# A fused attention and FFN kernel: batch 0 worked in token halves with gated loads, the first FFN block in halves, and the last output tile in two column pieces

## Chip, core and metric

The kernel runs on one core of one Trainium2 chip. The metric is the device time of one execution in microseconds (us); the median of several runs is compared. Profiles are of one execution each. Engines are named as in the profile: PE (matmul; PEld its weight loads), DVE (vector), ACT (scalar), POOL (GpSimd), SP (which issues most DMAs).

## What is computed

```python
# q, k, v: (8, 8, 576, 64); beacon_k, beacon_v: (8, 8, 16, 64)
k_all = concatenate([beacon_k, k], axis=2)        # 592 keys
v_all = concatenate([beacon_v, v], axis=2)
scores = q @ k_all.T / 8                          # beacons seen by all, the rest causal
a = softmax(scores)
attn = a @ v_all
x = attn.transpose(0, 2, 1, 3).reshape(4608, 512)
h = max(x @ w1, x @ w2, x @ w3)                   # each w: 512 x 768
out = h @ w_out                                   # 768 x 512, out 4608 x 512 f32
```

## The kernel before

**Units of work.** The work goes by pairs of heads, p = 0 to 31 (four pairs in each of eight batches), and two pairs make a quad (0 to 15). For a pair, q and k (f32) are loaded into a staging buffer `st` (nine of them, `load_pair`, line 161), cast to bf16 (`cast_pair`, line 192, mostly on POOL), and turned so that the head dimension lies on partitions: for the first four batches by PE transposes (`turn`, line 297, `turn_pair`, 344, `turn_apart`, 337), whose results are copied out of PSUM into `qT` and `kT` (`evac_q`, `evac_k`); for the last four by a store to DRAM and a transposing DMA. `place_beacons` (line 326) copies 16 turned beacon columns from `bT` into `kT`.

**Scores.** Keys lie in five tiles of 128 rows. `emit_scores` (375) does one of four groups of (key tile, query range) for both heads of a pair, into one of two score buffers in PSUM (`sc`, L385), and one exp on ACT writes `at_sb` (L394). No maximum is subtracted. `emit_masks` (398) clears what lies above the diagonal, by `affine_select` on POOL (L410) or by a product with a triangle `tri` on DVE (L408). Group 0 of every pair needs all of its keys' tiles 0 and 3, so a pair must be loaded and turned whole before its first score.

**PV.** `emit_pv` (430) multiplies for a quad and a token half (`hf`, 288 tokens each) the sums of `at` (with `ones`) and v, in two PSUM banks (`pv`, L451). `finish_pv` (462) inverts the sums by Ln and Exp on ACT (L469, L471) and multiplies into `xT` on DVE (L474). `xT` is a ring of four batches of x, turned. `ready` holds the last batch that is finished.

**FFN.** Blocks of 512 tokens; 22 units each. 18 units of `mm1_unit` (488; L497): one of three weights times one of six 128-wide pieces (`ft`) of the hidden size, four matmuls of 512 columns into an `fps` bank (two of them); DVE copies the first weight's result to `hT` (L505) and takes the maximum for the others (L507). Then 4 units of `mm2_unit` (509; L514): six matmuls, a copy to `y` (L522), and later a store (L529). Block 0 needs all of batch 0.

**Order.** There is no automatic schedule: instructions stand in each engine's queue as `emit_all` (672) writes them, and each engine goes through its own in order. `start` (587) issues the first loads, fills PE with matmuls on ones (`keep_busy`, L354) and turns pair 0. Pairs 0 to 4 are worked in four steps of one score group each with a list `fine_at` of what goes between; later pairs in two steps of two groups, with `plan` (`at_step`) giving POOL's casts, loads and weights. In each step `emit_ffn` may issue FFN units up to a limit that grows by 20/9 a step for nine steps and then by 2.75. 52 units are left when attention ends; they run alone on PE, alternating between the `fps` and `sc` banks, and the last four of them are the output tiles of block 8.

**Loads.** All but two pairs' k and one beacon load are issued by SP, in order; each cast is followed by the next load of the list `loads` (line 567). The weights are loaded and cast to bf16 by DMAs issued on POOL (`load_w`, L238; `load_w_out`, L243). Pairs 0 to 3 are laid out with nine tokens per partition row (2304 contiguous bytes), the later ones with six (1536 bytes); v comes in pieces of 256 bytes, one per token and head.

```python
    groups = [
        [(0, 0, HALF), (3, q_min[3], S)],
        [(0, HALF, S), (4, q_min[4], S)],
        [(1, q_min[1], S)],
        [(2, q_min[2], S)],
    ]
...
                if n_step <= 9:
                    allowed = 2 + n_step * (UPB - 2) / 9
                else:
                    allowed = (n_step - 1) * UPB / (2 * PPB)
```

Of the kernel before, what the change touches and what calls it, by code (L numbers as in the profile page):

```python
# [16 lines left out]
def kernel(  # L17
# [13 lines left out]
    nc = tc.nc  # L31
# [17 lines left out]
    PR = 9  # L49
    PP = S // PR  # L50
    P_NINE = 4
# [18 lines left out]
    groups = [  # L70
# [5 lines left out]
    NG = len(groups)  # L76
    g_width = [sum(q1 - q0 for _, q0, q1 in pieces) for pieces in groups]
    g_base = [2 * sum(g_width[:gi]) for gi in range(NG)]
    AT_W = 2 * sum(g_width)
    assert max(g_width) <= 512  # L80
# [9 lines left out]
    st_pool = ctx.enter_context(tc.tile_pool(name="st", bufs=9))  # L90
    pair_pool = ctx.enter_context(tc.tile_pool(name="pair", bufs=3))
    v_pool = ctx.enter_context(tc.tile_pool(name="v", bufs=2))
# [25 lines left out]
    make_identity(nc, ident)  # L118
# [7 lines left out]
    for i in range(NT):  # L126
        z = const.tile([128, NKP], BF16, name=f"kT{i}")
        nc.vector.memset(z[:, NK:NKP], 0.0)
        kTs.append(z)
    nc.vector.memset(ones, 1.0)  # L130
    tri = const.tile([128, 128], BF16, name="tri")
    nc.gpsimd.memset(tri, 1.0)
    nc.gpsimd.affine_select(
        out=tri,
        in_=tri,
        compare_op=ALU.is_ge,
        fill=0.0,
        base=0,
        pattern=[[1, 128]],
        channel_multiplier=-1,  # L140
    )
# [19 lines left out]
    def load_pair(p, k_queue=None):  # L161
        b, g, j0 = place(p)
        hs = slice(head(g, j0), head(g, j0) + 2)
        st = new_stage(("pair", p))
        for i, (src, queue) in enumerate(((q, nc.sync), (k, k_queue or nc.sync))):
            if p < P_NINE:
                queue.dma_start(
                    out=st[:, i * PR * D : (i + 1) * PR * D],
                    in_=src[b, hs].rearrange("h (p r) d -> (h p) (r d)", r=PR),
                )  # L170
            else:
                queue.dma_start(
                    out=st[0:QP, i * NQ2 : (i + 1) * NQ2].rearrange("p (h x) -> p h x", h=2),
                    in_=src[b, hs].rearrange("h (p r) d -> p h (r d)", r=QR),
                )

    def cast_piece(p, i, cast):
        st = stage["pair", p]
        if p < P_NINE:
            t16 = pair_pool.tile([128, PR, D], BF16, name=f"t16{i}")  # L180
            cast(
                t16.rearrange("x r d -> x (r d)"), st[:, i * PR * D : (i + 1) * PR * D]
            )
        else:
            t16 = pair_pool.tile([QP, QR, 2, D], BF16, name=f"p16{i}")
            cast(  # L186
                t16.rearrange("p r h d -> p h r d"),
                st[0:QP, i * NQ2 : (i + 1) * NQ2].rearrange("p (h r d) -> p h r d", h=2, r=QR),
            )
        stage["pair16", p, i] = t16  # L190
# [26 lines left out]
    def cast_v(b, piece, cast):  # L217
# [6 lines left out]
        while t < t_hi:  # L224
            t1 = t + 1
            while b > 0 and t1 < t_hi and k_rows[t1] == k_rows[t]:
                t1 += 1
# [5 lines left out]
            t = t1  # L233

# [19 lines left out]
    def turn_beacons(b0, b1, src):  # L254
        n = Nb * (b1 - b0)
        ps = ffn_psum.tile([128, PPB, n], BF16, name="fps")
# [40 lines left out]
    def turn(p, i, ps):  # L297
        src = stage.pop(("pair16", p, i))
        if p >= P_NINE:
            for r in range(QR):  # L300
                nc.tensor.transpose(  # L301
                    ps[:, r * QP : (r + 1) * QP],
                    src[:, r].rearrange("p h d -> p (h d)"),
                    ident[0:QP, 0:QP],
                )
            return
        for r in range(PR):
            for e in range(2):
                hs = slice(64 * e, 64 * e + 64)
                nc.tensor.transpose(  # L310
                    ps[hs, r * PP : (r + 1) * PP],
                    src[hs, r],
                    ident[hs, hs],
                    tile_position=(64 * e, 64 * e),
                )

    def rows(p):
        return PR if p < P_NINE else QR

    def evac_q(p, ps, copy):  # L320
        copy(
            qTs[p % NT].rearrange("d (p r) -> d p r", r=rows(p)),
            ps.rearrange("d (r p) -> d p r", r=rows(p)),
# [6 lines left out]
    def evac_k(p, ps, copy):  # L330
        kT = kTs[p % NT]
        copy(  # L332
            kT[:, Nb:NK].rearrange("d (p r) -> d p r", r=rows(p)),
            ps.rearrange("d (r p) -> d p r", r=rows(p)),
# [9 lines left out]
    def turn_pair(p, q_copy):  # L344
        banks = [pv_bank(i, [128, 1024], BF16) for i in range(2)]
        for i in range(2):
            turn(p, i, banks[i][:, 0:S])
        evac_q(p, banks[0][:, 0:S], q_copy)
        evac_k(p, banks[1][:, 0:S], by_dve)
# [12 lines left out]
    def at_view(p, t, e, q0, q1):  # L362
        for gi, pieces in enumerate(groups):
            off = g_base[gi] + e * g_width[gi]
            for t_, lo, hi in pieces:
                if t_ == t and lo <= q0 and q1 <= hi:
                    return at[p][0 : k_rows[t], off + q0 - lo : off + q1 - lo]
# [3 lines left out]
    def both_heads(p, gi):  # L371
        W = g_width[gi]
        return at[p][:, g_base[gi] : g_base[gi] + 2 * W].rearrange("k (e c) -> k e c", e=2)

    def emit_scores(p, gi):
# [6 lines left out]
        for t, q0, q1 in groups[gi]:  # L382
# [12 lines left out]
            out=both_heads(p, gi), in_=ps[:, :, 0 : g_width[gi]], func=AF.Exp, scale=scale  # L395
        )

    def emit_masks(p, gi, dve=False):
        off = 0
# [359 lines left out]
```

The softmax here doesn't subtract the row's maximum and nothing guards it: scores larger than these inputs give would overflow.

## Time and profile before

| what | us |
|---|---|
| five runs | 301.81, 303.73, 304.28, 303.27, 304.48 |
| median | 303.73 |
| the profiled execution, its time | 301.81 |
| its span, first to last instruction | 300.1 |
| busy: PE / DVE / ACT / POOL | 283.8 / 175.2 / 143.3 / 128.6 |
| first exp starts | 8.02 |
| first FFN matmul starts | 32.65 |
| transposes of pair 7 start | 47.63 |
| last matmul ends | 296.44 |

How to read it. The profile's page cuts the span in 40 slices of 7.5 us and gives for each the busy share of every engine in tenths, the clock that PE was granted, and the DMA engines' busy share. PE's busy time counts filler matmuls and matmuls at a lower clock as well, so 95% busy does not mean 95% useful. The timeline lists instructions with start and duration; "x12" means twelve in a row, and the time in square brackets is idle time before them and what ended it. The chain of waits goes back from the last instruction to what released each step. A duration of a DMA line on SPq is that of issuing it, not of the transfer.

### The profile page before, as it was taken

The numbers are of one execution on the slowest core, as the hardware profiler recorded it, in microseconds if no ns is written. First come the engines' busy times: TensorE is split into PE (matmuls) and PEld (weight loads), VectorE is DVE, ScalarE is ACT, GpSimd is POOL, SyncE is SP. The second block draws the span as 40 slices with busy tenths as digits, with TensorE's granted clock in tenths as the row PEclk, the third lists the DMA queues.
The fourth block names the chain that finished last, engine by engine and source line by source line (L and its number), as shares of the span: only waits on it lengthen the run. The fifth ranks groups of instructions, "written<-read, shape, count | busy, mean of one in ns | idle before, by whom it ended". The sixth has DMA issues, their size and how long they took to land.

```text
span 300.1 us, 8591 instructions
## 1 busy us (share of the span) xinstructions
PE 283.8 (95%) x3532; PEld 148.5 (49%) x3563; DVE 175.2 (58%) x330; ACT 143.3 (48%) x220; POOL 128.6 (43%) x261
## 2 busy tenths in 40 slices
PE   7798779999999999999999999999999999999995
PEld 4455235454544545454545777544454544444442
DVE  2868345656767465646564666465646575274373
ACT  3786466665555565536463646364635531400300
POOL 3876295465566683556355645552233210000000
PEclk9977799999999999999999999999999999999999
DMA  7999999999899999999998995376312001103003
GB/s 252 215 260 221 212 257 236 209 235 216 212 305 202 259 278 213 213 223 253 264 196 219 256 240 138 89 209 128 88 54 89 2 2 70 72 0 121 20 2 140
DMA packets 83095, 51.55 MB, mean 172 GB/s; under 512 B 62064, under 2 KB 76656, under 8 KB 83056
## 3 DMA queue, kind: packets, MB, share of 16 engines
q1 hardware_dynamic: 80976, 47.23, 68.1%
q0 software_dynamic: 1648, 3.15, 5.5%
q8 instruction: 28, 0.46, 0.7%
q10 hardware_dynamic: 432, 0.62, 0.7%
q14 instruction: 11, 0.09, 0.1%
HBM read 35.13 MB, written 14.22 MB: 164 GB/s over the span
## 4 chain that ended last, share of the span: by engine, by line
PE 80%; DMA 9%; SPq 3%; DVE 2%; POOL 2%; issue 2%; ACT 0%; POOLq 0%; DVEq 0%
PE fps L497 40%; PE fps L514 13%; PE pv L451 11%; PE sc L385 8%; DMA st<-in_v_dram 5%; PE sc L497 5%; PE sc L514 2%; DMA st<-in_q_dram 2%; DMA st<-in_k_dram 2%; SPq L213 1%; PE pv L301 1%; DVE kT L332 1%; POOL v_sb L229 1%; SPq L249 1%; POOL at_sb L410 1%
## 5 line engine op out<-in xcount | busy, mean ns | idle before, releaser
L394 ACT ACTIVATE at_sb<-sc 128x992 bf16<-128x992 f32 (+3 forms) x128 | 103.7, 862 | 98.4 <-PE sc L385 98.3
L497 PE MATMUL fps<-xT,w_sb 128*128 128x512 bf16 (+1 forms) x627 | 138.7, 358 | 3.1 <-issue 1.2
L497 PEld LDWEIGHTS <-w_sb 128*128 128x128 bf16 x720 | 65.9, 98 | 71.8 <-issue 16.0
L410 POOL TENSOR_SCALAR_AFFINE_SELECT at_sb<-at_sb 128x256 bf16<-128x256 bf16 (+2 forms) x145 | 52.7, 384 | 97.8 <-ACT at_sb L394 96.3
L507 DVE TENSOR_TENSOR hT<-hT,fps 128x512 bf16<-128x512 bf16 x96 | 65.7, 685 | 42.1 <-PE fps L497 41.9
L186 POOL CAST p<-st 96x768 bf16<-96x768 f32 x56 | 44.8, 825 | 1.1 <-DMA st<-in_k_dram 0.8
L505 DVE CAST hT<-fps 128x512 bf16<-128x512 f32 x42 | 29.0, 690 | 21.5 <-PE fps L497 21.4
L514 PE MATMUL fps<-w_out_sb,hT 128*128 128x512 bf16 x173 | 40.6, 379 | 1.0 <-issue 0.8
L385 PE MATMUL sc<-qT,kT 64*128 64x288 bf16 (+4 forms) x384 | 36.0, 285 | 1.4 <-DVE kT L332 0.8
L522 DVE COPY y<-fps 128x512 f32<-128x512 f32 x30 | 20.7, 689 | 27.9 <-PE fps L514 27.9
L514 PEld LDWEIGHTS <-hT 128*128 128x128 bf16 x216 | 20.5, 98 | 25.0 <-DVE hT L507 1.3
L451 PE MATMUL pv<-at_sb,v_sb 128*32 128x192 bf16 (+4 forms) x1352 | 29.0, 232 | 1.0 <-issue 1.0
L474 DVE TENSOR_TENSOR xT<-pv,recip 128x288 bf16<-128x288 f32 (+2 forms) x93 | 27.2, 347 | 4.3 <-ACT recip L471 4.3
L385 PEld LDWEIGHTS <-kT 64*128 64x128 bf16 x384 | 13.8, 94 | 26.9 <-issue 20.4
L451 PEld LDWEIGHTS <-v_sb 128*32 128x32 bf16 (+1 forms) x1408 | 25.1, 98 | 3.8 <-issue 2.4
L229 POOL CAST v_sb<-st 128x512 bf16<-128x512 f32 (+2 forms) x26 | 21.4, 840 | 9.5 <-DMA st<-in_v_dram 9.5
L451 PE MATMUL pv<-at_sb,ones 128*32 128x288 bf16 (+4 forms) x492 | 17.6, 260 | 1.2 <-POOL at_sb L410 1.1
L497 PE MATMUL sc<-xT,w_sb 128*128 128x512 bf16 x71 | 18.3, 379 | 0.1
L469 ACT ACTIVATE lnd<-pv 128x288 f32<-128x288 f32 x31 | 12.9, 416 | 7.0 <-PE pv L451 7.0
L451 PEld LDWEIGHTS <-ones 128*32 128x32 bf16 (+1 forms) x512 | 11.4, 98 | 8.4 <-issue 6.5
L507 DVE TENSOR_TENSOR hT<-hT,sc 128x512 bf16<-128x512 bf16 x12 | 8.2, 688 | 12.5 <-PE sc L497 6.8
L505 ACT CAST hT<-sc 128x512 bf16<-128x512 f32 x6 | 3.5, 585 | 23.7 <-PE sc L497 23.7
(47 smaller groups left out, 116.4 us busy)
## 6 DMA issues: line engine op xcount, KB each, us to landing
st<-in_q_dram SPq DMA_DIRECT2D x32, 288.0 KB, 5.1
out_dram<-y SPq DMA_DIRECT2D x36, 256.0 KB, 2.9
st<-in_k_dram SPq DMA_DIRECT2D x30, 288.0 KB, 5.6
st<-in_v_dram SPq DMA_DIRECT2D x24, 256.0 KB, 6.4
w_sb<-in_moe_w_dram POOLq DMA_DIRECT2D x6, 384.0 KB, 9.3
q_dram<-p SPq DMA_DIRECT2D x16, 144.0 KB, 3.2
k_dram<-p SPq DMA_DIRECT2D x16, 144.0 KB, 3.0
st<-in_v_dram SPq DMA_DIRECT2D x8, 224.0 KB, 6.5
```

What stands on the lines that cost most here:

```text
L186: cast(t16.rearrange("p r h d -> p h r d"), st[0:QP, i * NQ2 : (i + 1) * NQ2].rearrange("p (h r d) -> p h r d", h=2, r=QR),)
L229: cast(v_sb[0:n, t:t1].rearrange("p t h d -> p (t h d)"), st[0:n, (t - t_lo) * H * D : (t1 - t_lo) * H * D],)
L385: nc.tensor.matmul(ps[:, e, off : off + q1 - q0], kT[hs, 128 * t : 128 * t + 128], qT[hs, q0:q1], start=True, stop=True, tile_position=(64 ...
L394: nc.scalar.activation(out=both_heads(p, gi), in_=ps[:, :, 0 : g_width[gi]], func=AF.Exp, scale=scale)
L410: nc.gpsimd.affine_select(out=view, in_=view, compare_op=ALU.is_ge, fill=0.0, base=x0, pattern=[[0, 2], [1, hi - lo]], channel_multiplier=-1,)
L451: nc.tensor.matmul(ps[bank][32 * j : 32 * j + 32, lo + q0 - qa : lo + qb - qa], lhsT, at_view(PPQ * quad + j // 2, t, j % 2, q0, qb), star ...
L474: nc.vector.tensor_mul(xT[:, 2 * g + part - 1, c0 + ca : c0 + cb], ps[bank][:, lo : lo + cb - ca], recip[:, ca:cb],)
L497: nc.tensor.matmul(ps[:, o0 : o0 + n], w_in[i][:, ct, 128 * ft : 128 * (ft + 1)], xT[:, ct, x0 : x0 + n], start=(ct == 0), stop=(ct == n_c ...
L505: (by_act if alone[0] else by_dve)(hT[:, ft, :], ps)
L507: nc.vector.tensor_max(hT[:, ft, :], hT[:, ft, :], ps)
L514: nc.tensor.matmul(ps, hT[:, ft, 128 * tt : 128 * (tt + 1)], w_out_sb[:, ft, :], start=(ft == 0), stop=(ft == n_ft - 1),)
L522: nc.vector.tensor_copy(y, ps)
```

## The change

1. **Batch 0 in token halves.** q and k of batch 0 are loaded in halves of 288 tokens, with three tokens per row (768 contiguous bytes). The first half of pairs 0 and 1 comes in four f32 loads from SP and ACT, cast by DVE and ACT; the rest comes in six loads issued by POOL that cast to bf16 (`load_quad`: the first half of pairs 2 and 3, the second half of pairs 0 and 1, the second half of pairs 2 and 3). `turn_half` turns 288 tokens. The score groups of batch 0 are cut anew, so that group 0 needs the first half only, and PV's first half needs group 0 only.
2. **A written-out order of batch 0.** `first_steps` replaces `fine_at`: group 0 of all four pairs first, then the other groups of pair 0, 1, 2, 3, with turns, masks, PV, casts of v and FFN units between. The fillers in the steps are gone.
3. **Gated loads.** Loads of pairs 4 and 5 wait for a memset of one column by DVE; the loads behind them wait in SP's queue. SP's first loads are the halves and v of batch 0. The staging buffers are eight instead of nine.
4. **First FFN block in halves.** The first two weights of block 0 are done in units of two `ft` and 256 tokens; the first half needs only the first token half of batch 0 (`ready` counts halves now). 22 units as before; the limit grows from 6 at pair 4 to 22 in 11 steps, then by 2.75.
5. **The main loop.** The sums are inverted right behind PV's matmuls, the products come later (`multiply`). `turn_pair` stands in a pair's first step and uses a score buffer instead of the PV banks (from pair 6 on); `place_beacons` is done by DVE instead of POOL; the beacons' turn uses a score buffer; some FFN units use score buffers.
6. **The last tile.** The last output tile is computed as 320 and 192 columns, copied by ACT and DVE and stored in two DMAs.

```diff
+    groups_0 = [
+        [(0, 0, HALF), (1, q_min[1], HALF), (2, q_min[2], HALF)],
+        [(0, HALF, S), (3, q_min[3], S)],
+        [(1, HALF, S), (4, q_min[4], S)],
+        [(2, HALF, S)],
+    ]
...
-    st_pool = ctx.enter_context(tc.tile_pool(name="st", bufs=9))
+    st_pool = ctx.enter_context(tc.tile_pool(name="st", bufs=8))
...
+        if gate:
+            gate.memset(st[0:QP, 0:1], 0.0)
...
+    def load_quad(g, h):
+        for i in range(2):
+            t16 = const.tile([QP, 4, HR, D], BF16, name=f"quad{g}{h}{i}")
+            nc.gpsimd.dma_start(
+                out=t16.rearrange("p h r d -> p h (r d)"), in_=half_source(g, h, i, 0, 4)
+            )
...
+    def turn_half(p, h, pv, q_copy=None):
+        for i in range(2):
+            src = stage.pop(("half16", p, h, i))
...
+            for r in range(HR):
+                for e in range(2):
+                    nc.tensor.transpose(
+                        ps[64 * e : 64 * e + 64, r * QP : (r + 1) * QP],
+                        src[:, e, r],
+                        ident[0:QP, 0:QP],
+                        tile_position=(0, 64 * e),
+                    )
...
-    def turn_pair(p, q_copy):
-        banks = [pv_bank(i, [128, 1024], BF16) for i in range(2)]
+    def turn_pair(p, q_copy, shared=True):
+        if shared:
+            ps = sc_psum.tile([128, 2, 1024], BF16, name="sc")
+            banks = [ps[:, i, 0:S] for i in range(2)]
+        else:
+            banks = [pv_bank(i, [128, 1024], BF16)[:, 0:S] for i in range(2)]
...
+            if g == n_quad - 1 and n == len(passes) - 1:
+                ready[0] = 2 * b + hf
...
+    def mm1_halves(tb, ft, i, lo, hi, pool, name):
...
+        h = hTs[tb][:, ft : ft + 2, lo:hi]
+        ps = pool.tile([128, 2, MID], FP32, name=name)
...
+    def mm2_last(tb, tt, cuts):
...
+            (by_act if i % 2 == 0 else by_dve)(y[:, lo:hi], ps)
+            nc.sync.dma_start(out[c0 : c0 + 128, lo:hi], y[:, lo:hi])
...
     def start():
-        keep_busy(15)
-        next_load()
+        keep_busy(12)
+        load_half(0, 0, nc.sync)
+        load_half(0, 1, nc.scalar)
+        load_half(1, 0, nc.sync)
         load_beacons(0, 1, bk32_0, nc.scalar)
...
+        load_quad(1, 0)
+        load_quad(0, 1)
+        load_quad(1, 1)
+        next_load(3)
...
+    first_steps = [
+        ((0, 0), [T(2, 0, False)]),
+        ((1, 0), [M(0, 0, True), T(3, 0, True), V(0), V(1)]),
+        ((2, 0), [T(0, 1, False), V(2), L(load_w, 0, 0, d_ff)]),
+        ((3, 0), [T(1, 1, True), M(1, 0, True), M(2, 0, True)]),
+        ((0, 1), [M(0, 1)]),
+        ((0, 2), [T(2, 1, False), M(3, 0, True), M(0, 2), V(3), V(4)]),
+        ((0, 3), [M(0, 3, True), L(load_w, 1, 0, d_ff)]),
+        ((1, 1), [P(0, 0), M(1, 1)]),
+        ((1, 2), [T(3, 1, False), finish_pv, M(1, 2)]),
+        ((1, 3), [P(1, 0, True), M(1, 3, True)]),
+        ((2, 1), [finish_pv, G(4), cast_p]),
+        ((2, 2), [M(2, 1), M(2, 2, True)]),
+        ((2, 3), [P(0, 1, False, 0, 2), F(1), M(2, 3)]),
+        ((3, 1), [P(0, 1, False, 2, 4), M(3, 1, True), G(5), F(1), L(turn_beacons, 1, B_PE, bk16_1)]),
+        ((3, 2), [F(1), finish_pv, next_7, M(3, 2)]),
+        ((3, 3), [F(2), M(3, 3), L(cast_pair, 4, by_pool, by_pool), L(load_w, 2, 0, d_ff), P(1, 1),
+                  L(turn_apart, 4, 0), L(turn_apart, 4, 1), finish_pv, F(1), L(cast_pair, 5, by_pool, by_pool)]),
+    ]
...
-                if not fine and s == 0 and p + 1 < B_PE * PPB:
-                    place_beacons(p + 1, by_pool)
...
+                    if turned:
+                        place_beacons(p + 1, by_dve)
```

In `first_steps` each row is a score group (pair, group) and what is issued behind it: T(pair, half) a turn, M a mask (True: on DVE), V a cast of v, P(quad, half) PV, F(n) n FFN units, G a gated load.

## The prediction

> **What bounds the kernel now.** I read the 40 slices first, then the instructions in order of time for the first 60 us, then stretches of 3.4 us, then the chain of waits, and the end of the span last. In the slices PE is at 9 from the seventh on and the granted clock is full from the sixth on:
>
> ```profile
> PE   7798779999999999999999999999999999999995
> ...
> PEclk9977799999999999999999999999999999999999
> ```
>
> So the kernel has two parts: about 60 us in which PE is fed badly, and 236 us in which it has no room. Stretches of 3.4 us (columns: from:to, length, busy us and instructions of PE, of weight loads, of DVE, ACT, POOL, then clock, DMA share, GB/s) show the first part:
>
> ```profile
> 12.20:15.60 3.40, 1.43 (x12) 0.51 (x10) 3.40 (x8) 1.79 (x3) 2.13 (x5) 1.00 0.76 153
> 15.60:19.00 3.40, 3.40 (x58) 1.56 (x55) 1.05 (x6) 2.88 (x6) 1.91 (x4) 0.51 1.07 246
> 22.40:25.85 3.45, 2.11 (x56) 1.32 (x54) 3.45 (x8) 2.81 (x5) 2.66 (x5) 1.00 1.31 219
> 25.85:29.30 3.45, 3.45 (x85) 2.38 (x85) 2.77 (x9) 2.13 (x4) 2.04 (x5) 0.51 1.08 213
> 29.30:32.70 3.40, 1.60 (x57) 0.94 (x50) 0.89 (x3) 1.81 (x4) 0.00 (x0) 1.00 1.16 226
> 32.70:36.10 3.40, 3.18 (x7) 0.96 (x8) 0.69 (x1) 0.50 (x1) 0.13 (x1) 0.50 0.95 193
> 42.70:46.10 3.40, 2.46 (x45) 1.32 (x45) 0.69 (x1) 1.70 (x4) 2.88 (x8) 1.00 1.10 258
> ```
>
> After each stretch in which PE was 42 to 61% busy comes one at half clock; after one at 72% it does not. The first FFN matmul runs at 32.65, and the chain says what is late:
>
> ```profile
> 14.50 5.15 DMA st<-in_k_dram
> 19.67 16.15 DMA st<-in_v_dram
> ...
> 35.97 1.46 POOL v_sb L229
> ...
> 47.64 0.68 PE pv L301 x12
> ```
>
> Batch 1's v takes 16.15 us because pairs 4 to 6 and the first weights go through the DMA engines with it. The last line is my **marker**: the transposes of pair 7, at 47.63 in the timeline.
>
> How much is to be had: by 60.24 (half of pair 8's scores are out) PE has done 8.5 pairs of scores at 0.93 us (0.48 + 0.45 in the chain), three and a half quads of PV (0.79 + 1.61), 9 turned pairs (0.6) and 17 FFN units (0.87 for four matmuls): 7.9 + 8.0 + 5.4 + 14.8 = 36.1 us. 24.1 us are lost there. The same count for the rest (with 1.29 for a unit of six matmuls) gives 228 us of work in the 236 to the last matmul: 8 lost.
>
> **The change at the start: work.** To the marker the old order has 9 FFN units on PE (36 weight loads), all four score groups of pair 6, and pairs 0 to 6 turned. The new order has 12 units there (six in the written-out list, six in the main loop; each is half a block of two ft, 8 matmuls of 256 columns, the same 2048 columns), two groups of pair 6 (0.45 less), and the same PV and turns. At the marker it is 3 x 0.87 - 0.45 = 2.15 us ahead. 144 transposes become 96 and 27 filler matmuls 14; all lie in time in which PE waits for loads or for ACT, and I give them nothing.
>
> **When does the new marker come? By the DMA engines.** What must land before pair 7 is cast: the rows with 2304-byte pieces ran at 382 to 403 GB/s (4 to 8 us), v with its 256-byte pieces at 209 to 227 (9 to 12 us). Batch 0's q and k (2.36 MB) now come in 768-byte pieces, of which the trace has none: 5.9 us at 400, 11.2 at 210; I take 7.9 (300 GB/s), being nearer in size to the short row than to the long. Then: first byte 1.8, v of batch 0 5.5 (1.18 MB at 215), beacons 0.6, two of the four equal weights 8.2 (the POOL queue's line says 5.5% of the span for four, so 4.1 each), pairs 4 to 7 6.7 (2.36 MB at an estimated 350), v of batch 1 5.5. Sum 36.2; the third weight is issued amid v and adds up to 4.1: 40.3. Two casts at 0.82 follow: 37.8 to 41.9.
>
> ```profile
> q0 software_dynamic: 1648, 3.15, 5.5%
> ```
>
> **By ACT and PE.** The halves of pair 0 are 295 KB where the old first loads were 590; they should be there at 3.5 instead of 4.6, but filler runs to 4.7, the beacons' cast (now DVE) and pair 1's turn stand before the first scores, so the first exp starts near 7.0 (old 8.02). Then PE must wait, in order, for the quads: half clear of v, the three land near 7.7, 11.2 and 15 us (each 0.59 MB, v sharing). The second half of pair 2 is turned at 15; six exps are done by then. Left for ACT to the last exp of batch 0: 0.64 for (0,3) (the rows for 672 to 992 columns, continued to 576), three pairs at 1.00 + 0.78 + 0.64, three Ln and Exp at 0.86, a beacon copy 0.32: 10.8 us, so 26. Mask 0.4, casts of pair 4 1.65, evacuations 1.5 and one unit give pair 4's scores at 30. From there to the marker PE has 9.5 us (2.5 pairs of scores, PV 0.79, two turned pairs, 6 units) and ACT 10: 40. DVE has about 20 us of work from 3.5 to 30 (15 half evacuations at 0.44, between the 16- and 576-column rows, 16 masks at 0.24, casts, products, five units at 0.69), so it is not the bound. PE between 15 and 30 has 13 us (10 score groups 2.4, PV 4.8, two turns, 6 units); one or two stretches at half clock, which the gaps of 7 to 15 us invite, cost 1 to 2 beyond what ACT hides: 42.
>
> Both ways agree; I take **42**. The start gives 47.63 - 42 + 2.15 = 7.8 us. Ends: 37 (short pieces as fast as long ones, no half clock), giving 12.8; 48 (pieces at 210, three half-clock stretches, the weights late for their units), giving 1.8.
>
> The Trainium skill, "TensorE: Matmul & The Clock Gate", Part 1, throttles after at least one idle window of about 3.4 us; the rows above halve the clock after windows that were 42 to 61% busy. By the page the new start has no idle window and the marker would come at 40; the rows decide.
>
> **Waits and moves.** The two gates: pair 4's load waits for a one-column memset on DVE behind the products of quad 1, near 21 us; behind it on SP stand pairs 4 to 10 and v of batch 1. What covers it is that two weights (8.2 us) use the engines then; without that cover it costs the idle DMA time, up to 3 us, in the end 48. One staging buffer fewer delays only loads that run far ahead. On POOL the casts of pairs 1 to 3 go (6 x 0.66), six load issues come (0.53 each, as the weights' did); the first weight's loads now stand behind three casts of v, at about 16 us (old 20.48), and land near 23 (0.5 of issue, 4.1 and the rest of v, 2); the first unit wants them at 22.5.
>
> **The steady part.** PV sums are inverted at once, turns use the score banks and come a step earlier, some units use them too. PE loses about 0.3 us a pair there (0.17 before the scores, waiting for kT), so at most +3 for ten pairs. Against it, place_beacons moves from POOL (ten times 0.19) to DVE. This is what such a copy did beside POOL:
>
> ```profile
> 10.87 1.73 POOL L410 TENSOR_SCALAR_AFFINE_SELECT at_sb<-at_sb 128x224 bf16<-128x224 bf16 x5
> ...
> 11.57 2.17 DVE L328 COPY kT<-bT 128x16 bf16<-128x16 bf16 x1
> ...
> 12.55 1.16 POOL L229 CAST v_sb<-st 128x512 bf16<-128x512 f32 x2
> ...
> 15.37 0.15 DVE L328 COPY kT<-bT 128x16 bf16<-128x16 bf16 x1
> ```
>
> 0.15 us with POOL all but idle, 2.17 when POOL ran seven instructions without a gap until 13.71. Between 0 and 10 x 2.0 = 20 us of DVE time, which DVE's idle (0.2 to 2.8 us before each evacuation, 2 us a pair) mostly covers. I take -0.5 for the whole steady part, ends +3 and -6.
>
> The Trainium skill, "SBUF — State Buffer", Who interferes with whom, says that such a copy and a GpSimd instruction lock each other out for a whole instruction. By it a copy waits for one POOL instruction, at most about 1.5 us here; the row shows a wait across several, so I keep the row.
>
> **The tail.** Old: last matmul at 296.44, copy 0.69, store, 300.1.
>
> ```profile
> 296.47 0.69 DVE L522 COPY y<-fps 128x512 f32<-128x512 f32 x1 [0.61 <-PE fps L514]
> ```
>
> New: the last copy has 192 columns, about 0.34 (xT's 192-column row is 0.35), the store is 98 KB instead of 256, but PE does 12 weight loads (0.098 each) where it did 6, so the 192-column part runs at 0.6 rather than 0.48: +0.1. Net gain 0.3 (0 to 0.6).
>
> **Sum.** 7.8 + 0.3 - 0.5 = 7.6. The profiled execution took 301.81 (span 300.1), giving 294.2; it is the fastest of the five runs shown, whose median is 303.73, giving **296.1**.
>
> **Rivals.**
> - *Sooner*: the marker at 37, steady part level: gain 13, 290.7. For it: DMA at 369 to 403 GB/s in the first 8 us. Against: v shares from the start, and ACT's 13.8 us of exps stay. 0.22.
> - *The port*: DVE's copies reach PE at 0.6 us each in ten pairs: 7.8 + 0.3 - 6 = 2.1, so 301.6. For: the 2.17 row. Against: two FFN banks and DVE at 58%. 0.16 (0.10 of it still faster, 0.05 level, 0.01 slower).
> - *Quads late, slower*: batch 0 hangs on six casting loads in POOL's queue. If their price went by pieces and not by bytes (384 short ones each, where half a weight has 128 long ones in 2.06 us), each would take 6.2 us and the third quad would land at 2.3 + 37 = 39. Half way between that and 15, at 27, it is 12 late, and ACT's chain passes all of it on: 7.6 - 12, so 308.1. It decides from a third quad later than 24. Against: v's 256-byte pieces kept 209 to 227 GB/s. 0.12.
> - *It does little*: half clock through most of the first 30 us and pair 7 waiting for the DMA eat it: marker near 48 with a small steady loss, 303. 0.06, level.
>
> The forecast has 0.44 (gain 4 to 10, 294 to 300). Faster by over 0.5%: 0.44 + 0.22 + 0.10 = 0.76; within 0.5% (about what this kernel's measurement can tell from no change): 0.11; slower: 0.13. The range 290 to 303.5 leaves out the far end of *sooner* (0.08) and *quads late* (0.12).
>
> **What would show it.** First exp near 7; pair 2's second half turned near 15; pair 4's scores near 30; pair 7's transposes near 42 with 12 units done; the new DVE copy from bT at 0.15 to 1 us in the steady part; the last copy at 0.34. I am wrong if the six quad loads land after 20 us or before 11, if PE's clock stays full or stays halved through 30 us, or if PE is below 98% after 60 us.

## The result, and the profile after

The changed kernel takes 304.59 us (median of 53 runs, 303.47 to 307.47), the kernel before 303.7 (95 runs): the ratio is 1.0041, 95% interval [1.0029, 1.0053], so it is **1.2 us slower** (the medians are 0.9 apart), where 7.6 us less was forecast. The profiled execution of the changed kernel took 306.55 us (span 304.8), one of its slower ones, and that of the kernel before 301.81, one of its fastest. The two profiles are 4.7 us apart, and only a quarter of that is the change; so stages are compared below, and not ends.

The slices of the kernel after (busy share in tenths, granted clock in tenths):

```profile
PE   7899987999997999999999999999999999999994
...
PEclk9555999999999999999999999999999999999999
```

PE is busier than before from 22.5 to 45 us, but three slices (7.6 to 30.5 us) stand at half clock; the kernel before had three at 7 tenths (15 to 37.5 us). The stretches of 3.4 us, as in the prediction, show it closely (clock, DMA share and GB/s are the last three columns):

```profile
5.40:8.80 3.40, 1.79 (x30) 1.03 (x30) 2.70 (x8) 1.37 (x4) 0.55 (x1) 0.97 1.37 199
8.80:12.20 3.40, 2.83 (x42) 1.86 (x42) 2.29 (x9) 2.11 (x3) 1.18 (x2) 0.50 1.42 181
12.20:15.60 3.40, 3.32 (x44) 1.85 (x41) 2.73 (x10) 2.54 (x3) 0.90 (x3) 0.50 1.31 207
15.60:19.00 3.40, 3.36 (x60) 1.47 (x59) 1.94 (x6) 1.92 (x4) 3.27 (x7) 0.50 0.86 150
19.00:22.40 3.40, 3.40 (x66) 1.79 (x63) 1.86 (x6) 1.94 (x5) 2.01 (x5) 0.50 1.10 207
22.40:25.85 3.45, 2.67 (x47) 1.60 (x43) 1.04 (x5) 2.95 (x5) 0.73 (x2) 0.50 0.75 146
25.85:29.30 3.45, 3.45 (x53) 2.20 (x50) 0.69 (x1) 1.00 (x1) 0.00 (x0) 0.53 0.61 173
29.30:32.70 3.40, 3.40 (x35) 2.47 (x36) 2.05 (x6) 2.17 (x5) 0.32 (x1) 1.00 0.44 110
```

PE was 53% busy from 5.4 to 8.8, and then six stretches in a row are at half clock, though PE is 77 to 100% busy in them. The DMA share falls to 0.61 and 0.44 between 25.85 and 32.7. The chain of waits around the marker (start, duration, what), and then POOL's work ahead of the marker and the marker itself in the timeline:

```profile
30.01 1.11 SPq L180
33.72 2.96 SPq L245
...
37.96 4.66 SPq L245
42.66 1.73 SPq L180
44.44 6.60 DMA st<-in_k_dram
```

```profile
48.82 1.16 POOL L261 CAST v_sb<-st 128x512 bf16<-128x512 f32 x2
...
50.02 0.82 POOL L218 CAST p<-st 96x768 bf16<-96x768 f32 x1
...
50.91 0.43 PE L345 MATMUL sc<-ident,p 96*128 96x96 bf16 x6 [0.35 <-POOL p L218]
```

Pair 5's load is issued up to 31.1, then pair 6's, then SP takes ten microseconds to issue batch 1's v (L245), and behind it come pair 7's q (42.66) and k, which lands at 51.04. The marker is the turn of the q half, cast on POOL from 50.02, right behind two casts of v; the k half is turned at 52.07. The marker came at 50.9 instead of 42. By the prediction's own reckoning (marker before 47.63, 2.15 us of work ahead) that makes 50.91 - 47.63 - 2.15 = 1.1 us slower, and 1.2 was measured. How much this agreement is worth is said further down; the time of the marker is what missed.

### The profile page after: what moved, and what is told of

Read it like the earlier page. It is cut to its first block, busy times and chain, and to the rows that moved or that the text cites. A ratio compares the mean times of both kernels' runs of the same rounds, so it can differ in the third digit from the quotient of the medians.

```text
span 304.8 us, 8599 instructions
## 1 busy us (share of the span) xinstructions
PE 286.5 (94%) x3542; PEld 154.3 (51%) x3572; DVE 177.4 (58%) x357; ACT 145.0 (48%) x222; POOL 127.9 (42%) x253
## 4 chain that ended last, share of the span: by engine, by line
PE 76%; DMA 7%; SPq 6%; DVE 3%; issue 2%; POOL 2%; ACT 2%; POOLq 0%; DVEq 0%
PE fps L574 28%; PE sc L574 12%; PE pv L514 11%; PE fps L610 11%; PE sc L442 8%; DMA st<-in_k_dram 4%; PE sc L610 4%; SPq L245 4%; DMA quad<-in_k_dram 3%; SPq L180 2%; PE sc L345 1%; ACT at_sb L451 1%; POOL quad L209 1%; DVE xT L546 1%; DVE y L618 1%
## 5 line engine op out<-in xcount | busy, mean ns | idle before, releaser
L451 ACT ACTIVATE at_sb<-sc 128x928 bf16<-128x928 f32 (+5 forms) x128 | 104.0, 861 | 90.0 <-PE sc L442 89.0
L574 PE MATMUL fps<-xT,w_sb 128*128 128x512 bf16 (+1 forms) x464 | 106.4, 356 | 2.4 <-issue 0.8
L584 DVE TENSOR_TENSOR hT<-hT,fps 128x512 bf16<-128x512 bf16 x70 | 47.9, 686 | 31.0 <-PE fps L574 30.5
L574 PE MATMUL sc<-xT,w_sb 128*128 128x512 bf16 (+1 forms) x187 | 42.9, 356 | 0.1
L442 PE MATMUL sc<-qT,kT 64*128 64x288 bf16 (+5 forms) x400 | 38.1, 292 | 2.8 <-ACT at_sb L451 1.2
L584 DVE TENSOR_TENSOR hT<-hT,sc 128x512 bf16<-128x512 bf16 x32 | 22.0, 687 | 16.4 <-PE sc L574 10.6
L514 PE MATMUL pv<-at_sb,v_sb 128*32 128x288 bf16 (+5 forms) x1376 | 30.0, 234 | 0.0
L442 PEld LDWEIGHTS <-kT 64*128 64x128 bf16 x400 | 14.9, 97 | 28.1 <-issue 22.9
L261 POOL CAST v_sb<-st 128x1536 bf16<-128x1536 f32 (+2 forms) x21 | 18.4, 893 | 1.0 <-DMA st<-in_v_dram 1.0
L514 PEld LDWEIGHTS <-ones 128*32 128x32 bf16 (+2 forms) x512 | 11.2, 97 | 10.8 <-issue 9.1
L610 PE MATMUL sc<-w_out_sb,hT 128*128 128x512 bf16 x58 | 14.5, 379 | 0.3 <-DVE hT L584 0.3
```

Source lines behind the costliest of these rows:

```text
L261: cast(v_sb[0:n, t:t1].rearrange("p t h d -> p (t h d)"), st[0:n, (t - t_lo) * H * D : (t1 - t_lo) * H * D],)
L442: nc.tensor.matmul(ps[:, e, off : off + q1 - q0], kT[hs, 128 * t : 128 * t + 128], qT[hs, q0:q1], start=True, stop=True, tile_position=(64 ...
L451: nc.scalar.activation(out=both_heads(p, gi), in_=ps[:, :, 0 : g_width(p, gi)], func=AF.Exp, scale=scale)
L514: nc.tensor.matmul(ps[bank][32 * j : 32 * j + 32, lo + q0 - qa : lo + qb - qa], lhsT, at_view(PPQ * quad + j // 2, t, j % 2, q0, qb), star ...
L574: nc.tensor.matmul(ps[:, o0 : o0 + n], w_in[i][:, ct, 128 * ft : 128 * (ft + 1)], xT[:, ct, x0 : x0 + n], start=(ct == 0), stop=(ct == n_c ...
L584: nc.vector.tensor_max(h, h, ps)
```

## The experiments

Two theories to begin with. **A**: the clock, halved for 20 us, made batch 0 late. **B**: the gates made the loads late. **C** (DVE's copies beside POOL) and **D** (a late load of the last beacons at pair 12) are rivals for the rest. Ratios are to the kernel before, run beside each on the same chip (median 303.4 to 303.5 us); "fillers" are matmuls on ones. "Pair 4" is where its first scores start, "step 12" the time from pair 12's first scores to pair 13's.

| kernel | median us | ratio, 95% interval | pair 4 | marker | step 12 |
|---|---|---|---|---|---|
| before | 303.7 | 1 | - | 47.63 | 8.12 |
| changed | 304.59 | 1.0041 [1.0029, 1.0053] | 37.47 | 50.91 | 10.24 |
| e1 fillers | 302.5 | 0.9964 [0.9938, 0.9991] | 34.95 | 47.77 | 8.13 |
| e2 gates early | 302.65 | 0.9980 [0.9960, 1.0001] | 36.45 | 48.77 | 8.13 |
| e3 both | 300.82 | 0.9911 [0.9881, 0.9941] | 35.22 | 47.65 | 8.99 |
| e4 beacons' load early | 305.01 | 1.0042 [1.0012, 1.0071] | 37.69 | 50.84 | 8.58 |
| e5 = e3, fewer fillers | 301.0 | 0.9913 [0.9878, 0.9948] | 35.70 | 48.03 | 8.13 |
| e6 = e3, POOL places | 299.73 | 0.9895 [0.9859, 0.9931] | 35.37 | 46.70 | 9.25 |
| e16 = e6 again | 300.85 | 0.9915 [0.9890, 0.9940] | 34.94 | 46.17 | 9.13 |
| e7 = e3, last tile whole | 301.2 | 0.9943 [0.9918, 0.9969] | 35.34 | 47.66 | 8.13 |
| e8 = e3, POOL's order, `w_out` later | 302.61 | 0.9981 [0.9941, 1.0021] | 35.32 | 46.98 | 8.13 |
| e9 = e6, beacons early | 301.46 | 0.9943 [0.9918, 0.9967] | 35.40 | 46.91 | 9.46 |
| e10 = e6, units later | 303.49 | 1.0005 [0.9977, 1.0033] | 33.58 | 48.07 | 8.13 |
| e11 changed, ten fillers | 304.33 | 1.0039 [1.0010, 1.0068] | 38.24 | 51.34 | 9.76 |
| e12 before, eight fewer | 304.28 | 1.0039 [1.0016, 1.0062] | - | 51.15 | 8.13 |
| e13 = e6, nine buffers | 300.68 | 0.9915 [0.9882, 0.9948] | 35.16 | 47.22 | 8.65 |
| e14 = e6, turn first | 300.35 | 0.9902 [0.9871, 0.9933] | 35.82 | 47.20 | 8.13 |
| e15 changed, nine buffers | 304.48 | 1.0041 [1.0010, 1.0072] | 36.37 | 49.42 | 8.54 |

**e1 to e3: clock and gates.**

```diff
+        keep_busy(5)                              # e1: behind turn_half(0, 0)
...
-        ((0, 0), [T(2, 0, False)]),
+        ((0, 0), [T(2, 0, False, 5)]),            # 5 between its two turns
-        ((0, 1), [M(0, 1)]),
+        ((0, 1), [K(3), M(0, 1)]),                # and so on, 48 in all
...
-        ((1, 2), [T(3, 1, False), finish_pv, M(1, 2)]),
+        ((1, 2), [T(3, 1, False), G(4), finish_pv, M(1, 2)]),    # e2
-        ((2, 1), [finish_pv, G(4), cast_p]),
+        ((2, 1), [finish_pv, G(5), cast_p]),
```

Fillers alone: 

> The changed kernel with 48 filler matmuls in batch 0 (5 behind the first turn, 5 between the two turns of pair 2's first half, 2 or 3 in the next steps, 8 short ones behind two of the PV stretches); nothing else. Theory A (20 us of half clock from 8.8 to 29.3 made batch 0 late): the clock is full for most of 8.8 to 26, pair 4's scores come at 31 to 33 instead of 37.5, and the marker (pair 7's transposes, now 50.9) at 44 to 47, the time 299 to 301. Theory B (pair 7 waits for its load, which stands on SP behind the two gates, pair 6 and 10 us of v): the clock may be full, but the marker moves only as far as the first gate does (25.1 now); where the gate's memset comes 3 us earlier, the marker does too, and no more. If the fillers leave the clock at half, the marker stays and A is not tested.

Earlier gates alone: 

> The changed kernel with the two gates earlier in DVE's order: pair 4's ahead of the products of quad 0 (about 20 us instead of 25.1), pair 5's where pair 4's was (25 instead of 29.7); no fillers. Theory A: PE at half clock still brings pair 4's scores at 37 and 12 us more to the marker, so the marker comes at 49 to 50 and the time falls by 1 at most. Theory B: pair 6 and v of batch 1 start 5 us earlier, pair 7's load is issued at 38 instead of 42.7 and lands at 45 to 46; the marker comes at 46 and the time falls by 4 to 5.

Both: 

> The fillers and the earlier gates together. If A and B each hide behind the other (each alone worth 1 to 4 us), the marker comes at 42 to 43, where the prediction had it, and the time is 297 to 299. Theory A alone: the same as with the fillers alone. Theory B alone: the same as with the earlier gates alone.

The same work in the changed kernel and then with the fillers, twelve transposes and 32 matmuls of PV (start, duration):

```profile
12.83 0.69 PE L360 MATMUL pv<-ident,quad 96*64 96x96 bf16 x12
...
17.00 1.40 PE L514 MATMUL pv<-at_sb,v_sb 128*32 128x288 bf16 x32
```

```profile
13.50 0.45 PE L362 MATMUL pv<-ident,quad 96*64 96x96 bf16 x12
...
17.76 0.97 PE L516 MATMUL pv<-at_sb,v_sb 128*32 128x288 bf16 x32
```

48 more matmuls make the kernel faster: PE keeps its speed, pair 4 comes 2.5 us earlier and the ratio falls from 1.0041 to 0.9964, 2.3 us. The gates, without fillers, give 0.6% or 1.9 us (the interval reaches no change against before, but not 1.0041); PE is as slow there as in the changed kernel. With the early gates (e2) the DMA engines work through the hole: from 25.85 to 32.7 their share was 0.61 and 0.44 in the changed kernel, in e2 it is 1.08 and 1.14:

```profile
25.85:29.30 3.45, 3.45 (x62) 2.36 (x64) 1.01 (x3) 1.00 (x1) 0.00 (x0) 1.00 1.08 282
29.30:32.70 3.40, 3.40 (x38) 2.46 (x39) 2.75 (x7) 2.29 (x5) 1.16 (x3) 1.00 1.14 233
```

Together 1.3%, 3.9 us, about the sum. So both A and B cost time, each about half of these 3.9 us; but neither marker nor time reached what either had promised (the marker 46 for B, 42 to 43 for both), and e3 is still 4.7 us above the forecast.

**e4, e9, e13, e15: pair 12.** In the changed kernel's profile POOL waits 4.68 us for the beacons of batches 4 to 7, and step 12 takes 2.1 us more than before.

```diff
+        if b == B_PE - 1:                         # e4, e9
+            loads.append(lambda: [load_beacons(B_PE, B, bk32), load_pair(12)])
...
-    st_pool = ctx.enter_context(tc.tile_pool(name="st", bufs=8))
+    st_pool = ctx.enter_context(tc.tile_pool(name="st", bufs=9))    # e13, e15
```

> The changed kernel, with the loads of the beacons' keys of batches 4 to 7 issued by SP just ahead of pair 12's load instead of ahead of pair 16's; nothing else. Theory D (POOL's cast of these beacons waits 4.7 us for a load that SP issues at 83 instead of 75, and the masks of pair 12 stand behind it): the lag against the kernel before stays at 2.7 us from pair 12 to pair 13, where it grows to 4.6 in the changed kernel, and the time falls by 1.9, to 302.6 to 302.9. Rival (POOL or DVE is late there for another reason, the port or the y stores): the time stays at 304.6.

> All fillers, the earlier gates and POOL's placing of the beacons' columns, and in addition the load of the beacons of batches 4 to 7 ahead of pair 12's load. Theory D in its narrower form (POOL waits 3 to 4.7 us for these beacons in every kernel with the late load, but PE is held only where the wait is over about 3.3 us: 0.59 of idle PE and a step of 9.25 instead of 8.13 from pair 12 to 13 here): the step falls to 8.1 to 8.6 and the time by 0.5 to 1 from 299.7. Rival: POOL's wait is covered on the average and the time stays at 299.7.

> All fillers, earlier gates, POOL's placing, and nine staging buffers again (the four halves of pairs 0 and 1 lie in one of them, so that it fits). Theory J (with eight buffers loads come too late in the middle: POOL waits 3 to 5 us around 80 to 87 for whatever comes then, beacons or a pair, and PE loses 1.1 in the step from pair 12 to 13): POOL's wait there shrinks to under 2, the step takes 8.1 to 8.5 instead of 9.25, and the time falls by 0.5 to 1.2 against the same kernel with eight. Rival (SP's order, with y stores and 10 us of v ahead of these loads, sets it and not the buffers): the step stays at 9 or more and the time within 0.5.

> The changed kernel with nine staging buffers and nothing else. Theory J: the step from pair 12 to 13 takes 8.1 to 8.6 instead of 10.24 and the time falls by 0.5 to 1.5 from 304.6. Rival: the prediction's own price, nothing, is right, and the time stays at 304.2 to 305.

For nine buffers the four f32 halves of pairs 0 and 1 were moved into one of them (that part of the edit isn't printed here). POOL's wait for the beacons went in e4 and e9, and the time did not (1.0042; 0.9943 where e6 had 0.9895 and e16 0.9915). With nine buffers it stays as well (0.9915 beside e16's 0.9915; 1.0041 beside 1.0041). Step 12 did shorten as forecast in e4 (8.58) and e15 (8.54), but it also stood at 8.13 in e1, which changed nothing there. As accounts of the time, theory D and theory J fall. Step 12 lies between 8.13 and 10.24 from one kernel to the next and was still 9.46 in e9, where POOL stands idle for 4.2 us ahead of a pair's casts instead. What sets it stays open; at the median it can't be a large part of the loss, since kernels with 8.13 and with 9.1 have the same time (e5 and e16).

**e6, e16: the copies on DVE.**

```diff
-                        place_beacons(p + 1, by_dve)
+                        place_beacons(p + 1, by_pool)
```

> All fillers and earlier gates, and in the main loop the beacons' columns are placed by POOL again, as before the change. Theory C (the port: the copy of 16 columns on DVE beside POOL's casts took 1.90 us at 37.9 and held pair 5's scores 1.18 us; elsewhere 0.16 to 1.1): that stall of 1.18 goes, and the time falls by about 1. Rival: the copy then waits in POOL's queue behind masks and casts, pair 5's scores start no earlier, and the time stays or rises by up to 1.

> The kernel with all fillers, earlier gates and POOL's placing once more, on the same chip as the others of this set, since its 299.7 came from five runs and the same kernel with earlier beacons gave 301.5 on another chip. If POOL's placing is worth the 1.2 us that the trace shows at pair 5, it stays at 299.5 to 300.3; if not, it comes at 300.6 to 301.5, as with DVE's.

In the changed kernel, the three copies of pairs 4 to 6:

```profile
37.03 0.37 DVE L380 COPY kT<-bT 128x16 bf16<-128x16 bf16 x1
40.36 1.90 DVE L380 COPY kT<-bT 128x16 bf16<-128x16 bf16 x1
45.00 0.16 DVE L380 COPY kT<-bT 128x16 bf16<-128x16 bf16 x1
```

The stall at pair 5 went, and the marker came 1 to 1.5 us earlier; but e3, e6 and e16 have 0.9911, 0.9895 and 0.9915, and the repeat came where I had expected it if the copies cost nothing. At most some tenths of a per cent are in it.

**e5, e10, e14: what paces batch 0.**

```diff
-        ((2, 3), [P(0, 1, False, 0, 2), F(1), M(2, 3)]),          # e10: all six F out
+        ((2, 3), [P(0, 1, False, 0, 2), M(2, 3)]),
...
-                  P(1, 1), L(turn_apart, 4, 0), L(turn_apart, 4, 1), finish_pv,
+                  L(turn_apart, 4, 0), L(turn_apart, 4, 1), P(1, 1), finish_pv,     # e14
```

> The fillers only up to the step (0, 2), 28 of the 49, with the earlier gates; nothing else against the kernel with all fillers and earlier gates (pair 4's scores at 35.2, 300.8). Theory A2 (at full clock PE itself has no room from 17 to 33, since PV, units and scores there are 18 us and not 13, and the late fillers are in its way): pair 4's scores come 1.5 to 2.4 earlier, at 33 to 33.7, the time falls by at most as much, since POOL or the loads hold the marker at 46 to 47. Rival (ACT's exps set the pace): pair 4's scores stay at 35 and the clock may fall to half again after 17.

> All fillers, earlier gates, POOL's placing, and none of the six FFN units within batch 0's list: they come later, two a step, 22 by the same step. Theory F (at full clock PE's own work sets batch 0's pace from 16 on): five units of 0.96 go from ahead of pair 4's scores, which come at 30.5 to 31.5 instead of 35.4, and the time stays within 1 of 299.7, since the work is only moved. Rival G (ACT's exps or DVE's masks and copies set the pace): pair 4's scores come at 33 or later and the time rises by 2 or more, because the units filled time in which PE waits anyway.

> All fillers, earlier gates, POOL's placing, and pair 4 is turned ahead of the last PV of batch 0 instead of behind it; nothing else. Theory K (pair 4's turn stands on PE behind a PV that itself waits until Ln, Exp and the products of the PV before have freed its banks, and then 1.9 us of evacuations and beacons on DVE): the turn starts at 31.4 instead of 33.1, PE does PV while DVE evacuates, the 0.59 of idle PE goes, and pair 4's scores start at 34.0 to 34.8 instead of 35.4; the time falls by 0.5 to 1.2. Rival (PE's work is only put in another order, and the marker hangs on POOL): the time stays within 0.4.

e5 has 27 of the 48 fillers (the count in its expectation is off by one). Without the late ones PE slowed down again at 22.7 (20 matmuls of PV 1.15 us instead of 0.68), behind a stretch in which it was 72% busy, and pair 4 came no earlier; so the theory that the late fillers are in the way fell, or was at best hidden by the clock.

```profile
19.00:22.40 3.40, 2.44 (x66) 1.54 (x65) 2.34 (x9) 2.81 (x5) 1.97 (x5) 1.00 1.09 211
22.40:25.85 3.45, 3.15 (x46) 2.02 (x46) 1.04 (x5) 2.20 (x5) 0.73 (x2) 0.53 1.07 231
```

With the units out (e10), 4.8 us of PE work less brought pair 4's scores only 1.8 us earlier, and the time rose by 1.1% against e6 (0.9% against e16). PE then waits (the square brackets), and is slow again behind the wait (the turn 1.14 us instead of 0.68):

```profile
29.21 0.68 PE L516 MATMUL pv<-at_sb,ones 128*32 128x288 bf16 x20 [2.23 <-DVE xT L548]
...
33.58 0.90 PE L444 MATMUL sc<-qT,kT 64*128 64x288 bf16 x8 [1.37 <-DVE kT L382]
```

The last PV of batch 0 waits until Ln, Exp and products of the one before have freed its banks, and pair 4's turn stands behind it. The six units fill this. How much of the loss is the waiting and how much the slow PE behind it isn't separated. That PE's work alone sets the pace is refuted, even if the slow turn is allowed for. e14 puts the turn ahead and gains nothing either: the 0.59 us of idle PE goes, but the turn now waits for POOL's casts and pair 4 comes at 35.8.

**e11, e12: how few fillers, and what the old ones did.**

```diff
+        keep_busy(5)                              # e11: only these ten
-        ((0, 0), [T(2, 0, False)]),
+        ((0, 0), [T(2, 0, False, 5)]),
...
-        (1, 2): [L(keep_busy, 2, 320, True)],     # e12: and (1, 3), (2, 2), (2, 3)
```

> The changed kernel with only the ten fillers that cover the two waits before 9 us, in the stretch 5.4 to 8.8 where PE was 53% busy; nothing else. Theory H (each stretch is judged by itself, and a batch 0 without fillers keeps PE under about 70% at full clock): PE is at full speed until 12.2 or 15.6 and halves again, 12 transposes of half a pair take 0.45 at 10 and 0.69 at 14 to 19, pair 4's scores come at 36 to 37, and the time falls by under 1 from 304.6. Rival I (the first stretch alone puts the clock down, and it then stays there because work at half clock is too thin to bring it back): the clock is full to 22 and more, pair 4's scores at 34.5 to 35.5 as with all fillers, the time 302 to 302.8.

> The kernel before without the eight fillers of its steps (those between 14 and 20 us); nothing else. If these eight fillers carry the clock, as theory A has it for the changed kernel: PE is at half speed for most of 12 to 29 instead of two stretches, the first FFN unit comes 1 to 2.5 later than 32.65 and the time is 304.5 to 306. If the fillers do nothing there (PE waits for loads, v of batch 1 lands at 35.8 in any case): the time stays within 0.7 of 303.5.

e11: PE is 98% busy from 5.4 to 8.8, then 60% busy, and the next stretch is slow again:

```profile
8.80:12.20 3.40, 2.03 (x44) 1.28 (x42) 2.22 (x9) 2.00 (x3) 0.61 (x1) 1.00 1.41 181
12.20:15.60 3.40, 2.49 (x38) 1.39 (x32) 2.65 (x10) 2.69 (x3) 1.13 (x2) 0.54 1.24 205
```

Theory H holds for the clock, though pair 4 comes at 38.2 and not at 36 to 37, and the gain is nothing that shows. e12: eight fillers fewer cost the kernel before 0.39% [0.16, 0.62], 1.2 us. They looked like dead weight in its profile and were worth that.

**e7, e8: the tail, and POOL's order.**

```diff
-        while done[0] < END - 1 and emit_ffn(END, *tail[i % 2]):    # e7
+        while emit_ffn(END, *tail[i % 2]):
...
-        mm2_last(n_tokb - 1, TOKB // 128 - 1, (0, 320, 512))
...
-    at_step(5, 0, L(load_w_out))                  # e8: to (6, 0); pair 7's casts ahead of v's
```

> All fillers and earlier gates, and the last output tile in one piece, as before the change. The prediction's tail: two pieces gain 0.3, so from the first matmul of the last tile to the end of the span it takes 5.6 to 5.9 in one piece against 5.3 now, and the time rises by 0.3. Rival, from the profiles: two pieces take 5.3 to 5.7 where the kernel before took 5.13, so one piece is 0.2 to 0.5 faster.

> All fillers and earlier gates, and on POOL pair 7's casts go ahead of the last two casts of v of batch 1, and the load of the last weight moves a pair later. Theory E (with the loads early, POOL's queue holds the marker: it runs without a gap from 41.6 to 48.4, pair 7's casts at 46.8 behind 2.6 us of v and 0.85 us of issuing a weight): the marker comes at 45.3 to 46 instead of 47.65 and the time falls by 0.5 to 1.5, unless PV of batch 1 then waits for v. Rival (PE and ACT set the pace there): the marker comes earlier by under 0.5 and the time stays.

From the first matmul of the last tile to the end of the span it takes 5.3 to 5.7 us in the kernels with two pieces, 5.1 in the kernel before and 5.4 in e7: no difference that the runs can tell, in the time either. In the changed kernel the last copy did shrink as forecast, but what follows it did not:

```profile
300.67 0.82 SPq L638 DMA_DIRECT2D out_dram<-y  x2
300.71 0.36 DVE L637 COPY y<-sc 128x192 f32<-128x192 f32 x1 [0.62 <-PE sc L630]
```

From the end of the last copy (301.07) to the end of the span are 3.73 us, where the kernel before had 2.94 with a store of 512 columns. e8 brought the marker 0.7 us earlier, a third of what theory E had promised, and lost 0.7%. Its trace shows where the time can go: the other half of the edit, the later load of `w_out`, makes PE wait for it, and the six matmuls behind the wait take 2.73 us instead of 1.46.

```profile
62.22 2.73 PE L612 MATMUL fps<-w_out_sb,hT 128*128 128x512 bf16 x6 [0.73 <-DMA w_out_sb<-in_moe_w_out_dram]
```

So e8 doesn't tell what the earlier casts alone are worth in time.

## Why the prediction was wrong

**The frame held only roughly.** A badly fed start, a saturated rest, the marker, and 2.15 us of work ahead of it: marker minus 47.63 minus 2.15 gives +1.1 for the changed kernel (measured +1.2), -2.0 for e1 (-1.1), -2.1 for e3 (-2.7), -3.6 for e16 (-2.6). This sets markers of single executions against ratios of many, and that the first agrees to 0.1 us is in part luck: for e12, with no work ahead, the marker says +3.5 where +1.2 was measured. Nor does the lead show at its size within the profiles. From the marker to the last matmul the kernel before took 248.8 us; 2.15 less would be 246.7, but e1 took 247.6, e3 248.1, e16 248.3 and the changed kernel 249.8, 2.1 of it in step 12. The six loads that were the *quads late* rival landed in pairs at 7.4 and 8.9, 11.0 and 11.9, 13.2 and 14.9, close to what I had taken (7.7, 11.2, 15).

**The step that failed is "By ACT and PE"**, from "the second half of pair 2 is turned at 15" (14.43, right) to "pair 4's scores at 30" (37.5). Two terms of it were mis-sized; from there to the marker, where it had 10 us, the changed kernel took 13.4 and e16 11.2.
- "One or two stretches at half clock, which the gaps of 7 to 15 us invite, cost 1 to 2 beyond what ACT hides": it was six, up to 29.3, which comes close to its own sign of being wrong, a clock that "stays halved through 30 us". Undoing them (e1) gave 2.3 us. The rows that the prediction quoted said that a stretch under about 61% busy halves the next. I used them for the gaps, but not for what stands between them: with the gaps filled in e11, transposes and 64-row scores at full speed leave PE 60% busy in the next stretch. The rows were also read too sharply: "after one at 72% it does not" meets a 72% in e5 after which it did, and in e12 a stretch at 60% (29.3 to 32.7) after which the clock stayed full. And the 27 old fillers, 14 in the new order, "I give them nothing": eight of them are worth 1.2 us in the old kernel.
- "Left for ACT to the last exp of batch 0 ... 10.8 us, so 26" takes ACT as never waiting. The work itself was summed right, 11.0 us in e16, but even at full speed ACT waits for scores there:

```profile
19.02 0.78 ACT L453 ACTIVATE at_sb<-sc 128x736 bf16<-128x736 f32 x1 [0.61 <-PE sc L444]
...
22.10 1.00 ACT L453 ACTIVATE at_sb<-sc 128x992 bf16<-128x992 f32 x1 [0.99 <-PE sc L444]
...
26.17 1.00 ACT L453 ACTIVATE at_sb<-sc 128x992 bf16<-128x992 f32 x1 [1.08 <-PE sc L444]
27.96 0.32 ACT L310 COPY bT<-sc 128x192 bf16<-128x192 bf16 x1 [0.80 <-PE sc L303]
...
29.66 0.63 ACT L453 ACTIVATE at_sb<-sc 128x576 bf16<-128x576 f32 x1
```

Its gaps from 15 on add up to some 4 us, and the last exp ends at 30.3, not 26; in the changed kernel at 32.8. PE is busy for 15.04 of these 15.29 us in e16, up to 3.1 of them with fillers, so keeping the clock up this way is not free. PE, ACT and DVE hand each other work in order, and each queue holds PV, units or masks ahead of what the next one wants. Adding the busy time of one engine gives the earliest end, not the likely one. That this is the remaining 4 to 5 us is argued from these gaps and from e10 and e14, which show that neither PE's work nor the place of one turn sets it; no variant of the changed kernel brought pair 4's scores ahead of 33.6, so it isn't shown by removing it.

**The gates.** Their price was right as a bound ("without that cover ... up to 3 us") and wrong as taken (nothing). Pair 4's gate opened at 25.0 instead of "near 21"; the two weights that were to cover it had landed by 26.8. Half clock isn't the reason: with full clock (e1) it opened at 24.8, since the products ahead of it wait for ACT's inverted sums, which stand behind an exp that waits for scores (rows of e1):

```profile
22.12 1.00 ACT L453 ACTIVATE at_sb<-sc 128x992 bf16<-128x992 f32 x1 [0.99 <-PE sc L444]
...
23.93 0.89 DVE L548 TENSOR_TENSOR xT<-fps,recip 128x288 bf16<-128x288 f32 x3 [2.27 <-ACT recip L538]
...
24.76 0.06 DVE L178 MEMSET st<- 96x1 f32 x1
```

Only pair 5's gate came markedly earlier with the clock, at 27.5 instead of 29.6. So half clock and late gates are two errors, and they add up; e2 gives 1.9 us for the gates.

**"Both ways agree; I take 42"** was the weak place: both sums left out what each engine waits for, so their agreement said nothing. *It does little* had the mechanism, half clock through most of the first 30 us and pair 7 waiting for the DMA, with the marker near 48; it was put at 0.06.

**Right at their size:** one staging buffer fewer, nothing (e15). In the steady part the DVE copies cost nothing that the time shows, though one took 1.90 us where 0.15 to 1 was forecast; the term's -0.5 itself isn't shown, since the stretch behind the marker was longer than reckoned in every profile above. **Wrong, but small:** the tail's +0.3 is nothing; three and a half quads of PV at 2.40 are 8.4 us and not 8.0; and "382 to 403 GB/s" passes over a row of 333 (5 to 6 us). Nothing in the forecast's miss hangs on these.

The weighing of the Trainium skill's rule ("TensorE: Matmul & The Clock Gate", Part 1, a throttle after an idle window) against the rows came out for the rows: PE slowed after windows 53% (changed kernel) and 60% (e11) busy, with no idle window.

## What to carry to other kernels

Before a change thins PE's work or drops fillers, work out PE's busy share in each 3.4 us stretch at full speed; where it falls to about 60%, price half clock for the stretches that follow, and keep fillers there; in this case the border wasn't sharp (60% was once harmless, 72% once not). A load that is gated on an engine's progress starts when that engine's queue gets there, so price what the instructions ahead of the gate wait for (here it opened 4 us later than reckoned). A sum of one engine's busy time is a lower end for when it finishes: with in-order queues that feed each other, waits come on top (here 4 us on 11, in one kernel).

## What the runs showed of the hardware

**PE stays slow though busy.** In the changed kernel five stretches of 77 to 100% busy at half clock didn't bring the clock back; behind the one in which the first eight FFN matmuls (128 rows by 128 columns) ran it was full, at 29.3. That it was these matmuls isn't shown: in e12 the clock came back at 26.2 behind PV, scores and turns alone. In the kernel before one slow stretch, with fillers, PV or FFN, was enough.

**The recorded clock can miss it.** In e2's profile the clock is given as full throughout, yet PE is as slow as in the changed kernel:

```profile
12.74 0.69 PE L360 MATMUL pv<-ident,quad 96*64 96x96 bf16 x12
...
16.91 1.40 PE L514 MATMUL pv<-at_sb,v_sb 128*32 128x288 bf16 x32
```

```profile
15.60:19.00 3.40, 3.28 (x61) 1.56 (x62) 1.14 (x5) 1.83 (x4) 3.40 (x8) 1.00 0.71 122
```

0.69 and 1.40 are the half-clock durations of above. Of the executions of the changed kernel 28 have a mean recorded clock over 0.99 (median 304.45 us) and 26 under 0.98 (304.92): the same kernel, 0.5 us apart. The speed of PE is read from the durations of like matmuls; the clock row only confirms it.
